# Folding two masks into one, moving q's diagonal copies to GpSimd, and taking eps out of the normalizations' chain

## The chip, the core and the metric

The kernel runs on one core of one Trainium2 chip. A core has a matrix engine (TensorE, PE in the profile; PEld is its weight load), a vector engine (VectorE, DVE), a scalar engine (ScalarE, ACT), GpSimd (POOL), and SyncE (SP), whose queue here issues nearly all DMAs. Each engine takes its instructions in program order; an instruction that waits for a semaphore holds everything behind it on that engine. The metric is the device time of one execution in microseconds; the median of the runs counts.

## What is computed

One transformer block on x of 2048 rows and 448 columns: a normalization modulated by c, attention with 16 heads of 28 columns in a sliding window of 256 keys, a residual, a second modulated normalization, and a gated MLP whose gate mixes all rows (w_sp) after a normalization of its own. Cut to what matters:

```python
def _layernorm(x, axis=-1, eps=1e-05):
    m = jnp.mean(x, axis=axis, keepdims=True)
    v = jnp.var(x, axis=axis, keepdims=True)
    return (x - m) / jnp.sqrt(v + eps)
...
    # A: B, S, D = 1, 2048, 448; H = 16; Dh = 28; W = 256
    scores = jnp.einsum('bhqd,bhkd->bhqk', q, k) * Dh ** (-0.5)
    mask = (idx[:, None] - idx[None, :] >= 0) & (idx[:, None] - idx[None, :] < W)
    scores = jnp.where(mask[None, None], scores, -1000000000.0)
    o = jnp.einsum('bhqk,bhkd->bhqd', _softmax(scores, axis=-1), v)
    return merge_heads(o) @ wo
...
    # B: Fh = 896
    z = _gelu(jnp.einsum('bsd,df->bsf', x, w_in))
    z2 = _layernorm(z[..., Fh:], axis=-1)
    g = jnp.einsum('ts,bsf->btf', w_sp, z2) + b_sp[None, :, None]
    return jnp.einsum('bsf,fd->bsd', z[..., :Fh] * g, w_out)
...
    h = _layernorm(x, axis=-1) * (1 + ca) + sa
    x = x + ga * _A_ref(h, A_wqkv, A_wo)
    h = _layernorm(x, axis=-1) * (1 + cb) + sb
    x = x + gb * _B_ref(h, B_w_in, B_w_sp, B_b_sp, B_w_out)
```

## The kernel before

Rows are tiled by 128 (16 tiles, j or t), and four tiles are a token block (tb 0 to 3). The work of every tile is written as small operations with their dependencies; a class `Sched` holds them. The order is not found at run time: a long string, `PLAN`, lists every operation by number with its engine (p for PE, a for ACT, d for DVE, t for POOL, s for SP) and its buffer slots. `order()` walks it and appends each operation to its engine's program; `waits()` then derives the semaphore waits. The string is one list for all engines, so the place of a word says only what stands before it on the same engine.

The first normalization and Q, K, V (per token block): `stats` runs `bn_stats` (L626) and `bn_aggr` (L629) on DVE, adds eps on DVE or POOL (L631, into `ve_all`), and takes the power -1/2 on POOL (L633, `rs_all`). `norm` normalizes on DVE (L644) or on POOL (L649 the negated mean times rsqrt, into `ve_all` again; L651). SP transposes the result by DMA into `hT` (L467), L732 applies the modulation, and PE makes q (L763; L797 for block 0), k (L821) and v (L841). q is copied from PSUM to `qT` (L772, L773; L802, L803 for block 0). Then four copies per token block put q's heads on a block diagonal, `QBD` (L790 on ACT and L791 on DVE; L815 and L816 for block 0). Each copy writes 32 partitions. They wait for the zeroing of QBD (L521) as well.

Attention for tile j has two halves of 8 heads, each with three key blocks: the middle one needs no mask, the two others (the edges) do. Since they are complementary, they are folded into one 160-column strip per head. The scores of a half go to four PSUM banks (L956), one exponential moves them to `PW` (L912), and DVE multiplies the folded edges by the 0/1 mask into `PT` (L975). This is one operation for four heads, `mask_all(k)`, so two for each half. The scores of 64 further columns of the middle block come from QBD, L967, once per tile. PV (L1003) for four heads, k = 0 or 1 of a half, needs the mask of its k. L1017 and L1019 divide, SP transposes, L1029 multiplies by wo, L1033 adds x, and the second normalization follows for each tile: `stats` with slot 1, `norm` with a copy of the last columns (L656, L657), a transpose by DMA and the modulation (L1052, L1054).

The MLP: L1123 and L1144 are the two parts of x @ w_in, with gelu on ACT (L1130, L1152); z2's normalization uses `stats` with slot 2 (two bn_stats per tile) and L1135. L1168 is w_sp @ z2, L1172 and L1175 the gate, L1187 the output product, L1197 the last residual.

The columns of the folded edges for the two k of a half, before, with `PWT` = 576 columns per PSUM bank's worth:

```python
at_m0, at_f, at_hm = ((0, (128, 288), 448), (384, (64, 224), 0))[j % 2]
...
cols(hp.slot[0] * 2048 + 1024 * k, [[256, 4], [128, 2], [1, 128]]), cols(at_w() + pad + at_f[k], [[PWT, 4], [32, 2], [1, 128]], PW),
cols(0, [[0, 4], [128, 2], [1, 128]], mask01[:].rearrange("p b q -> p (b q)")), ALU.mult), [exs[0]] + t_mask, v - 7.0 + k)
```

Of the kernel before, what the change touches and what calls it, by code (L numbers as in the profile page):

```python
# [12 lines left out]
d24 d22 p47.1 p56.3 p48.2 p55.0 p57.1 p59.0 a0 a3 a5 a7 a9 d23 p37.1 p65.2 p71.3 p61.1 p49.0 p64.2 p50.3 p73.0  # L13
p46.3 p67.0 s1 s2 s4 d110 s6 s10 s8 a38 p42.0 p43 p44.1 p45 p70.2 p72.1 p60.2 t27 t28 t29 t32 t33 t30 d108
d111 t31 d109 t112 t113 t34 a100 t26 t102 t35 d115.3 d114.2 p124.7 d83 d82 p127.0 p75.0 a128 a129 d103 d125
d126 d118 d119 d116 d117 a104 p80.1 p77.0 p78.1 p76.2 p74.0 p52.3 p69.2 p68.0 s12 d182 d180 p62.1 t101 p51.0
p148.1 p81.2 p139.5 p140 p149 a150 p79.1 p54.2 a141 t106 t107 t105 p136.7 p137 a138 p63.2 t120 t121 d123.2
d122.0 p133.3 p130.6 p66.3 p53.0 p145.0 p146 p58.2 a131 d176 d183 d134 a135 s13 d243 d178 d177 d181 d179 t25
d184 t185 t191 t187 t189 d245 d41 d241 d186.3 s11 p142.7 p372.0 a132 p163.1 p170.6 p171 d244 p164 d165 a147
p151.0 p143 d144 d172 d247 p152 d153 a373.0 p378.0 p154.1 p155 d156 a39 a379.4 p397.0 a398.1 a399 a169 t36  # L20
d382 d374 d246 d166 d376 p157.7 p158 a159 s15 p90.1 p91 d92 d248 d84 d85 d242 d400 p93.0 p94 d95 d380 s193
t188.1 s194 t190.2 s195 t192.0 s196 d197 d200 p404.0 a405.5 p173.1 p174 a175 p160.7 p161 p375.0 p86.0 p87 d88
d198 d89 a406 a40 p425.0 a426.6.0 t249 t250 t254 d407 t252 t199 p377 p381 p383 d409 d384 d402 t253.2 d162
p217.0 p218 a219 a168 p210.1 p211 d212 p433.0 a434.0 p201.0 p202 a203 d167 p204.1 p205 a206 s14 d310 d385.2
p401.0 p403 p453.0 a454.2.1 s16 d430 s849 s259 t255.1 s260 d251.0 d256 d429 d436 d312 s386 s258 t257.3 s261
t97 t96 t262 t99 t263 t265 p226.0 p427.0 a428 p207.1 p227 p408 p208 d228 d306 p410 d411 d412.1 d307 s413 d98
d311 d435 a209 d215 d458 p461.0 p229.0 a462.1 d464 d214 d463 d457 p220.1 p221 p230 a231 p431.0 p432 s851
p481.0 p437 p438 d439 p223.0 p224 d225 d313 p455.0 a222 p232.1 d440.2 s441 d213 a482.3.2 d486 p489.0 d308 p233
d234 p235.0 p236 a456 a216 p483.0 p459.0 p460 a490.0 p508.0 d491 d492 d309 s21 s17 s852 p465 p466 d467 d485
d468.0 s469 a237 t264 p387.0 p388 d389 p414.1 p415 a484 p510.0 d416 t314 t315 a509.6.0 p536.0 a511 d390 d512  # L30
d391 p487.0 p488 p493 p494 p272.0 p538.0 d495 d496.1 a537.2.1 d541 d513 d540 p273 a274 p516.0 a517.5 p269.1
p275.0 p276 d277 p270 d271 p514.0 p515 a539 p564.0 a565.3.2 p282.0 p266.1 p267 a268 d519 p283 p566.0 a567 a284
d518 p520 t319 t320.1 s325 t321 t322.2 s326 d316.0 s323 t317 t318.3 s324 t330 d280 d417 d569 p544.0 a545.1
p442.1 p443 d444 d281 p521 d522 d523.0 p288.0 p289 a290 p291.1 p292 a293 p572.0 a573.5 p238.0 p239 d279 p294.1
p542.0 p295 p543 p592.0 a240 p470.0 p471 d445 d446 d546 d418 d419 d278 s20 s497 s848 s524 t392 t393 d547
d394.2 t395 s396 a296 a593.4.0 d568 p548 p549 p285.1 p594.0 p286 a287 p600.0 a601.2 d575 d472 p300.0 p301 a302
d550 d551.1 p570.0 p571 d596 d574 d473 p576 p577 p619.0 t420 t329 t327 d328 d597 p525.1 p337.0 p526 d578
d579.0 p598.0 a595 p599 p338 d603 d474 d527 a620.3.1 p627.0 d602 d528 d475 d421 d529 d530 t531 t447 t476
t422.0 t532 p340.1 p341 a339 s552 p553.0 p554 s18 p604 p605 a628.5 p647.0 a648.6.2 p621.0 a622 d342 p498.1
p499 d555 p297.0 p298 a299 t477 d606 d607.2 d623 p625.0 d624 s853 s580 s608 d500 t423 s424 d652 d556 d630 d557  # L40
d629 d501 t448 t449 t450.1 t451 s452 p675.0 a676.0.0 d680 p626 p334.0 p335 a336 p331.1 p332 a333 d651 d345
t478.2 d479 s480 p655.0 a656.1 p609.0 p610 p649.0 a650 p347.1 p348 p631 a349 d611 d612 d346 d657 d679 d344
p683.0 a684.2 p632 p677.0 d633 d502 p350.0 p351 a352 p359.1 p360 d558 t559 t560 t561.0 t822 t503 d634.2 s635
p703.0 d658 d686 d533.2 p303.0 p304 d305 d685 s19 p653.0 p654 p659 p660 d661 d823 t562 d662.0 s663 t534 s535
t504 t824 t821 d505.1 t506 s507 a704.5.1 p711.0 a361 p353.1 p354 d343 d355 a678 d707 d613 a712.1 d714 d708
p681.0 p365.0 p366 a367 p730.0 a731.3.2 p682 p687 p688 p705.0 a706 d713 d689 d690.2 s691 p356.1 p357 p581.0
a358 d735 d734 p738.0 a739.2 p732.0 a733 p582 d583 d584 p709.0 p710 p715 d740 p716 d717 d718.0 s719 s563 d585
t586 p664.0 p758.0 a759.0.1 p368.1 p369 a370 d741 p665 d666 t587 d588 t589.2 d762 d667 p736.0 p737 p742 p766.0
# [12 lines left out]
d835 t834 d939 d913 d833 d914 d902 d967 d954 d923 d955 d974 d975 t940 t897 d898 d947 t933 d934 t903 t904 d949
# [44 lines left out]
class Op:  # L106
    def __init__(self, n, ways, deps, prio, take, table, dma, lat, tail):
# [1160 lines left out]
```

## Time and profile before

| | |
|---|---|
| median of 3 runs | 282.59 us (282.34 to 283.21) |
| span of the profiled execution, first to last instruction | 279.0 us |
| what lies around the span, median less span | 3.6 us |
| PE, DVE, ACT, POOL busy | 267.3, 164.5, 121.4, 127.3 us |
| the chain that ended last: PE, DVE, POOL, DMA | 53%, 21%, 12%, 7% |
| start of the L1168 stage on the chain | 158.10 us |

The profile lists only the span of its execution, so the time around it is taken from the median. A group's row has the engine's line, the operation, its output and inputs, how often, busy time and mean ns of one, and then the idle time ahead of it with what ended that. A row of a timeline has the start, the time from the first start to the last end of a run of equal instructions, and what it is; in square brackets the idle time ahead. A row of the chain has the start and the share of the chain. DVE's instructions overlap by some 70 ns at their ends, so the distance from start to start is what one costs in a full queue.

### The profile page before, as it was taken

How to read it: one execution, taken by the hardware profiler on the slowest of the kernel's cores; microseconds unless marked ns; L12 is line 12 of the kernel's file. 1: busy time of each engine (PE TensorE's matmuls, PEld its weight loads, DVE VectorE, ACT ScalarE, POOL GpSimd, SP SyncE). 2: the span in 40 equal slices, each digit the busy share in tenths (PEclk: the TensorE clock that was granted, in tenths of full speed). 3: DMA queues.
4: the chain of work that ended last, by engine and by line, in shares of the span. 5: the costliest groups of instructions: out<-in, count | busy, mean ns of one | idle time of the engine just before them, and what ended most of it. 6: DMA issues, size and time to landing. Idle time of an engine off the chain costs nothing.

```text
span 279.0 us, 8426 instructions
## 1 busy us (share of the span) xinstructions
PE 267.3 (96%) x3741; PEld 155.6 (56%) x3751; DVE 164.5 (59%) x377; ACT 121.4 (44%) x142; POOL 127.3 (46%) x182
## 2 busy tenths in 40 slices
PE   7899998998999799999989899999999999999995
PEld 5786686677668676544545444444444444454552
DVE  3698999978999999938879501120212012153143
ACT  2399998899699789466755500000000000000000
POOL 7554567617364831596576503155363024062320
PEclk9999999999999999999999999999999999999999
DMA  7997953956632343659489996000000000102013
GB/s 203 294 238 136 147 100 97 121 93 97 126 62 50 98 80 61 179 89 150 99 153 192 212 182 130 0 0 0 2 1 0 0 2 0 33 16 62 0 39 115
DMA packets 67302, 25.55 MB, mean 92 GB/s; under 512 B 58497, under 2 KB 66178, under 8 KB 67266
## 3 DMA queue, kind: packets, MB, share of 16 engines
q1 hardware_dynamic: 66304, 24.21, 43.6%
q10 hardware_dynamic: 962, 0.80, 1.1%
q8 instruction: 29, 0.48, 0.7%
q14 instruction: 7, 0.06, 0.1%
HBM read 9.01 MB, written 1.84 MB: 39 GB/s over the span
## 4 chain that ended last, share of the span: by engine, by line
PE 53%; DVE 21%; POOL 12%; DMA 7%; ACT 3%; issue 2%; SPq 1%; POOLq 0%; DVEq 0%
PE ps L1168 34%; DVE PT L975 8%; PE ps L1187 8%; POOL rs_all L633 5%; DMA hT<-xn 5%; DVE st_all L626 3%; DMA wmodA<-in_w_mod_dram 2%; DVE o_sb L1019 2%; DVE x_sb L1033 2%; PE ps L763 2%; POOL hT L1054 2%; POOL ve_all L631 2%; PE ps L956 1%; PE ps L821 1%; PE ps L841 1%
## 5 line engine op out<-in xcount | busy, mean ns | idle before, releaser
L1175 POOL TENSOR_TENSOR z1T<-tmpg,z1T 128x512 bf16<-128x512 bf16 x28 | 32.0, 1152 | 74.5 <-DVE tmpg L1172 74.5
L1172 DVE TENSOR_TENSOR tmpg<-ps,bsp_bc 128x512 bf16<-128x512 f32 x28 | 19.0, 689 | 75.6 <-PE ps L1168 64.3
L912 ACT ACTIVATE PW<-ps 128x2048 bf16<-128x2048 f32 (+1 forms) x42 | 60.0, 1454 | 6.8 <-PE ps L956 5.2
L1168 PE MATMUL ps<-wspB,z 128*128 128x512 bf16 x219 | 49.7, 379 | 0.3
L1168 PE MATMUL ps<-wspA,z 128*128 128x512 bf16 x219 | 49.1, 379 | 0.9 <-DVE z L1135 0.7
L975 DVE TENSOR_TENSOR PT<-PW,mask 128x1024 bf16<-128x1024 bf16 x56 | 38.6, 714 | 0.1
L1168 PEld LDWEIGHTS ps<-wspA,z 128*128 128x128 bf16 x224 | 21.8, 98 | 27.2 <-DVE z L1135 1.0
L1168 PEld LDWEIGHTS ps<-wspB,z 128*128 128x128 bf16 x224 | 21.9, 98 | 26.2
L633 POOL TENSOR_TENSOR rs_all<-ve_all,neghalf 128x1 f32<-128x1 f32 (+2 forms) x37 | 24.5, 670 | 19.4 <-DVE ve_all L631 18.3
L1003 PE MATMUL ps<-Vaug,PT 128*128 128x32 bf16 x496 | 23.4, 177 | 1.3 <-DVE PT L975 0.7
L1003 PEld LDWEIGHTS ps<-Vaug,PT 128*128 128x128 bf16 x496 | 21.5, 96 | 3.9 <-DVE o_sb L1019 1.0
L1123 PE MATMUL ps<-w_in,hT 64*128 64x448 bf16 x224 | 22.0, 349 | 1.2 <-DVE st_all L626 1.2
L1144 PE MATMUL ps<-hT,w_in 64*128 64x512 bf16 x196 | 22.2, 376 | 0.0
L1187 PE MATMUL ps<-w_out_g,z1T 128*128 128x448 bf16 (+2 forms) x119 | 22.0, 342 | 0.0
L626 DVE BATCH_NORM_STATS2 st_all<-x_sb 128x6 f32<-128x448 bf16 x32 | 19.5, 617 | 3.0 <-DMA x_sb<-in_A_x_dram 2.8
L626 DVE BATCH_NORM_STATS2 st_all<-z 128x6 f32<-128x448 bf16 x32 | 18.5, 610 | 3.7 <-ACT z L1130 3.6
L1003 PE MATMUL ps<-Vaug,PW 128*128 128x32 bf16 x224 | 19.8, 176 | 0.0
L821 PE MATMUL ps<-hT,WQK 112*128 112x128 bf16 x256 | 17.4, 219 | 1.3 <-DVE KT L834 1.0
L1197 DVE TENSOR_TENSOR fin<-ps,x_sb 128x448 bf16<-128x448 f32 (+2 forms) x17 | 9.8, 595 | 14.7 <-PE ps L1187 9.9
L1003 PEld LDWEIGHTS ps<-Vaug,PW 128*128 128x128 bf16 x224 | 17.5, 96 | 1.1
L956 PE MATMUL ps<-qT,KT 32*128 32x128 bf16 (+5 forms) x1344 | 17.1, 197 | 1.0 <-DVE KT L834 0.9
L1130 ACT ACTIVATE z<-ps 128x896 bf16<-128x896 f32 x16 | 13.9, 914 | 9.3 <-PE ps L1123 6.8
(104 smaller groups left out, 361.8 us busy)
## 6 DMA issues: line engine op xcount, KB each, us to landing
out_dram<-fin SPq DMA_DIRECT2D x15, 112.0 KB, 1.7
wmodB<-in_w_mod_dram SPq DMA_DIRECT2D x1, 1568.0 KB, 14.9
x_sb<-in_A_x_dram SPq DMA_DIRECT2D x3, 448.0 KB, 9.0
w_in<-in_B_w_in_dram SPq DMA_DIRECT2D x3, 448.0 KB, 4.5
w_out_g<-in_B_w_out_dram SPq DMA_DIRECT2D x1, 784.0 KB, 5.0
bsp_bc<-in_B_b_sp_dram SPq DMA_DIRECT2D x1, 512.0 KB, 5.2
x_sb<-in_A_x_dram SPq DMA_DIRECT2D x2, 224.0 KB, 5.1
hT<-xn SPq DMA_TRANSPOSE x28, 3.2
```

The source lines that it names most:

```text
L626: st = [dve(0.62 if True else 0, lambda e, t=t, ci=ci, s=s: e.bn_stats(st_all[:, slot, t, ci, :], s()), deps(t), prio) for ci, s in enumer ...
L633: return pool(0.4 + 0.15 * len(tiles), lambda e: e.tensor_tensor(rs_all[:, slot, a:b], ve_all[:, slot, a:b], neghalf[:, 0:b - a], ALU.pow) ...
L821: km = lambda g, kc, start, stop, h=h, t=t: lambda e: e.matmul(ps[:, h.slot[0], g * 128:(g + 1) * 128], lhsT=WQK[0:CP, kc, 16 + 4 * g:20 + ...
L912: ex = act(xdur, lambda e, out_ap=out_ap, in_ap=in_ap: e.activation(out_ap(), in_ap(), ACT.Exp, scale=SCALE), [s] + list(after), v - 8.0 + ...
L956: fm.append(lambda e, hm=hm, qi=qi, key=key, kn=kn, lo=lo, hi=hi, col=col, p0=p0, t=t, j=j: e.matmul(ps[p0:p0 + kn, hm.slot[t], col:col + ...
L975: return lock_d(0.68, lambda e: e.tensor_tensor(cols(hp.slot[0] * 2048 + 1024 * k, [[256, 4], [128, 2], [1, 128]]), cols(at_w() + pad + at ...
L1003: fns.append(lambda e, hp=hp, hO=hO, hi=hi, bi=bi, kb=kb, hd=hd, nb=nb, a=at[hi][bi], p_of=p_of: e.matmul(ps[:, hO.slot[0], 32 * hd:32 * h ...
L1123: return lambda e, kc, p0, start, stop: e.matmul(ps[:, hs[t % 2].slot[hf], 0:D], lhsT=hT[p0:p0 + 64, kc, t * 128:(t + 1) * 128], rhs=w_in[ ...
L1144: return lambda e, kc, p0, start, stop: e.matmul(ps[:, hs[b // 2].slot[b % 2], :], lhsT=w_in[p0:p0 + 64, kc, ft * 128:(ft + 1) * 128], rhs ...
L1168: m = pe(16 * MMS, [lambda e, h=h, si=si, ft=ft, tb=tb: e.matmul(ps[:, h.slot[0], :], lhsT=z2[:, si, ft * 128:(ft + 1) * 128], rhs=(wspA i ...
L1175: u = pool(1.16, lambda e, ht=ht, ft=ft, tb=tb: e.tensor_tensor(z1T[tb][:, ft, :], tmpg[:, ht.slot[0], :], z1T[tb][:, ft, :], ALU.mult), [ ...
L1187: return [lambda e, ft=ft: e.matmul(ps[:, h.slot[0], 0:hi - lo], lhsT=z1T[t // 4][:, ft, (t % 4) * 128:(t % 4 + 1) * 128], rhs=w_out_g[:, ...
```

## The change

Four edits, and the plan that goes with them.

1. The columns of the folded edges are laid out so that k = 1 lies half a `PWT` behind k = 0 for every bank, and one operation masks all eight heads of a half (128x2048). Both PV of a half wait for it. In the plan it stands in DVE's order where the later one of the two stood, among the same neighbours.
2. `lock_q` lets POOL do the copies to QBD, and the plan gives it the 13 that DVE did; the 3 on ACT stay. As these write 32 partitions, on POOL each such copy waits for the end of the operation before it, and the operation after it waits for the copy (`part`).
3. `st_all` has three more numbers for each normalization, a constant group of zero count and zero mean, and D x eps or Fh x eps as the sum of squares. `bn_aggr` takes it in (9 numbers for 6, or 15 for 12), so its variance has eps in it already; L631 and `ve_all` are gone, and L633 reads bn_aggr's result. Three memsets on DVE at the start write the constants.
4. The negated mean has a tensor of its own, `nm_all`.

The programs of PE, ACT and SP have the same instructions in the same order. On POOL the copies stand: the first ahead of block 1's three L651 and the second between block 2's; for block 1 three of them between the third and the fourth of block 2's L732 (the first copy of that three waits for q on ACT and DVE); for block 2 four of them behind the first of block 3's L732 and ahead of the next L633; for block 3 one ahead of an L651 of the second normalization, two behind it, and the last one behind a run of L1054 and L657.

```diff
+        self.part = False
...
+            prog = self.prog[op.eng]
+            if op.eng == "pool" and prog and (op.part or prog[-1].part):
+                op.deps.add(prog[-1])
+            prog.append(op)
...
-    st_all, _, _ = alloc("st_all", [128, 3, NT, 2, 6], F32)
+    st_all, _, _ = alloc("st_all", [128, 3, NT, 15], F32)
-    ve_all, _, _ = alloc("ve_all", [128, 3, NT], F32)
+    nm_all, _, _ = alloc("nm_all", [128, 3, NT], F32)
...
+    t_eps = [dve(0.1, lambda e: e.memset(st_all[:, :, :, 12:14], 0.0), prio=-98.0),
+             dve(0.1, lambda e: e.memset(st_all[:, 0:2, :, 14:15], D * EPS), prio=-98.0),
+             dve(0.1, lambda e: e.memset(st_all[:, 2:3, :, 14:15], FH * EPS), prio=-98.0)]
...
-            aggr.append(dve(0.2, lambda e, t=t, n=n: e.bn_aggr(mv_all[:, slot, t, :], st_all[:, slot, t, 0:n, :]), st, prio - 0.01))
+            aggr.append(dve(0.2, lambda e, t=t, n=n: e.bn_aggr(mv_all[:, slot, t, :], st_all[:, slot, t, 12 - 6 * n:15]), [st, t_eps], prio - 0.01))
-        fe = lambda e: e.tensor_scalar(ve_all[:, slot, a:b], mv_all[:, slot, a:b, 1], EPS, None, ALU.add)
-        ve = add({"dve": (0.16, fe), "pool": (0.23, fe)}, aggr, prio)
-        return pool(0.4 + 0.15 * len(tiles), lambda e: e.tensor_tensor(rs_all[:, slot, a:b], ve_all[:, slot, a:b], neghalf[:, 0:b - a], ALU.pow),
-                    [ve, t_nh], prio - 0.01)
+        return pool(0.4 + 0.15 * len(tiles), lambda e: e.tensor_tensor(rs_all[:, slot, a:b], mv_all[:, slot, a:b, 1], neghalf[:, 0:b - a], ALU.pow),
+                    [aggr, t_nh], prio - 0.01)
...
     def lock_q(*a):
-        return locks(either(*a))
+        op = locks(free(*a))
+        op.part = True
+        return op
...
-                at_m0, at_f, at_hm = ((0, (128, 288), 448), (384, (64, 224), 0))[j % 2]
+                at_m0, at_f, at_hm = ((160, (0, 288), 448), (224, (64, 352), 0))[j % 2]
...
-                def mask_all(k, hp=hp, at_w=at_w, pad=pad, at_f=at_f):
-                    return lock_d(0.68, lambda e: e.tensor_tensor(
-                        cols(hp.slot[0] * 2048 + 1024 * k, [[256, 4], [128, 2], [1, 128]]), cols(at_w() + pad + at_f[k], [[PWT, 4], [32, 2], [1, 128]], PW),
-                        cols(0, [[0, 4], [128, 2], [1, 128]], mask01[:].rearrange("p b q -> p (b q)")), ALU.mult), [exs[0]] + t_mask, v - 7.0 + k)
-                mks = [mask_all(k) for k in range(2)]
+                mk2 = lock_d(1.2, lambda e, hp=hp, at_w=at_w, pad=pad, at_f=at_f, cols=cols: e.tensor_tensor(
+                    cols(hp.slot[0] * 2048, [[256, 8], [128, 2], [1, 128]]), cols(at_w() + pad + at_f[0], [[PWT // 2, 8], [32, 2], [1, 128]], PW),
+                    cols(0, [[0, 8], [128, 2], [1, 128]], mask01[:].rearrange("p b q -> p (b q)")), ALU.mult), [exs[0]] + t_mask, v - 7.0)
+                mks = [mk2, mk2]
...
-                    at = [[(0, 1024 * k + 256 * hi), (1, PWT * hi + at_m), (0, 1024 * k + 256 * hi + 128)] for hi in range(4)]
+                    at = [[(0, 512 * hi + 256 * k), (1, PWT * hi + at_m), (0, 512 * hi + 256 * k + 128)] for hi in range(4)]
```

The durations in these lines (0.68, 1.2, 0.25 and so on) are the planner's costs, not measurements.

More of the change, by code (lines that the diff above doesn't have):

```diff
@@ L77 @@
+s1070 d1075.0 t1088 p1077.5 s1034 d1123.1 d1066.3 t1124 d1030.2 s1031 d1120.1 t1121 d1078.1 t1079 p1041.4
+d1042.1 s1043 d1036.1 s1067 s1037 p1080.7 p1089.5 p1083.0 d1081.1 t1082 d1084.1 t1115 p1139.2 p1038.1 t1085
+p1135.4 d1090.0 t1091 s1076 d1039.0 s1040 p1140 d1141.0 s1142 p1143.0 p1144 d1145.2 s1146 p1098.3 p1101.6
+d1102.0 d1099.1 s1100 s1103 p1131.5 p1132 p1136 d1133.3 s1134 p1071.2 d1137.0 d1072.2 s1073 s1138 p1104.5
+d1105.3 s1106 p1107.3 d1108.1 s1109
 """
@@ L647, in norm @@
         else:
-            nm = ve_all[:, slot, t:t + 1]
+            nm = nm_all[:, slot, t:t + 1]
             fm = lambda e: e.tensor_scalar(nm, m, z, -1.0, ALU.mult, ALU.mult)
```

129 lines of the change are left out of this document (60 added, 69 removed).

## The prediction

> **What bounds the kernel now.** I read the page's busy table by slices first, then the busy time by stages, then the chain of work that ended last, then the timelines around the points that the change touches. The slices are 7 us each:
>
> ```profile
> DVE  3698999978999999938879501120212012153143
> ACT  2399998899699789466755500000000000000000
> ```
>
> VectorE (DVE) is full from slice 3 to 15 and ScalarE (ACT) nearly so. The stages, cut where the chain changes its engine, say how full each engine is (time, then PE, PE's loads, DVE, ACT, POOL):
>
> ```profile
> 28.20:35.00 6.80, 6.80 (x157) 4.25 (x155) 6.26 (x15) 6.75 (x8) 3.68 (x4) 1.00 1.07 134
> 35.00:56.20 21.20, 20.18 (x621) 15.09 (x618) 20.97 (x43) 18.82 (x19) 14.24 (x16) 1.00 0.62 105
> 75.20:97.70 22.50, 20.94 (x660) 15.94 (x657) 21.61 (x46) 18.93 (x20) 15.15 (x21) 1.00 0.31 66
> 114.40:158.10 43.70, 41.77 (x407) 20.63 (x405) 34.98 (x98) 27.34 (x42) 30.91 (x60) 1.00 0.78 142
> ```
>
> From 28.2 to 35.0 TensorE (PE) has no gap: what starts it late there is lost. From 35.0 to 56.2 DVE is busy 20.97 of 21.20 us and bounds; PE (20.18) and ACT (18.82) are close, so relief of DVE can give 1 or 2 us there, not more. The same holds from 75.2 to 97.7. From 114.4 PE bounds with 1.9 us of gaps, and the last 121 us are PE alone, which the change doesn't touch.
>
> **The change part by part.** The instruction order on PE, ACT and SP is the same before and after. DVE's and POOL's differ. The prices:
>
> ```profile
> L975 DVE TENSOR_TENSOR PT<-PW,mask 128x1024 bf16<-128x1024 bf16 x56 | 38.6, 714 | 0.1
> L996 DVE TENSOR_TENSOR PT<-PT,mask 128x512 bf16<-128x512 bf16 x8 | 3.0, 400 | 0.0
> L791 DVE COPY QBD<-qT 32x512 bf16<-32x512 bf16 x11 | 3.8, 345 | 1.4 <-ACT qT L772 1.2
> L816 DVE COPY QBD<-qT 32x256 bf16<-32x256 bf16 x2 | 0.4, 200 | 0.0
> L631 DVE TENSOR_SCALAR ve_all<-mv_all 128x1 f32<-128x1 f32 x14 | 1.9, 142 | 0.1
> L631 POOL TENSOR_SCALAR ve_all<-mv_all 128x1 f32<-128x1 f32 x18 | 5.9, 334 | 7.4 <-DVE mv_all L629 7.0
> L629 DVE BATCH_NORM_AGGREGATE mv_all<-st_all 128x2 f32<-128x6 f32 x32 | 5.2, 170 | 0.3
> L629 DVE BATCH_NORM_AGGREGATE mv_all<-st_all 128x2 f32<-128x12 f32 x16 | 2.7, 186 | 0.0
> L615 POOL COPY WQK<-wq_st 112x448 bf16<-112x448 bf16 x5 | 2.7, 559 | 2.1 <-DMA wq_st<-in_A_wqkv_dram 2.1
> L657 POOL COPY xn<-xn x13: 231/238/2659, 65.1 to 136.5; 128x64 bf16<-128x64 bf16 x13
> ```
>
> *One mask for two.* No row shows 128x2048. From 512 to 1024 elements a mask grows by 314 ns (714 - 400), so the part that doesn't grow is 86 ns, and 2048 elements should take 714 + 2 x 314 = 1342 ns, against 2 x 714 for the pair: 86 ns x 28 = 2.4 us less. The bounds are 0 (all of it grows) and 28 x 400 ns = 11 us (a whole small mask is fixed), and below nothing if the longer pattern loses speed, which no row gives a reason for. I take 2 us, nearest to the line through both rows, spread evenly from 32 to 113 us. That the first half of a pair comes some 0.6 us later I cost at nothing: PE's program runs each PV some us behind its masks, and that other work covers it. Without the cover it would be 28 x 0.6 us at the most. [...]
>
> *q's diagonal copies.* 13 copies leave DVE: 11 x 345 + 2 x 200 ns = 4.2 us. On POOL two rows give a line: 64 elements in 238 ns, 448 in 559, so 0.84 ns an element, and 512 elements take 0.61 us, 256 elements 0.40. Each also waits for the operation before it on POOL, and the next one for it: some 0.1 us, as between dependent POOL operations below. POOL has room for 8 us in sum. But its queue is in order, so the place of each copy decides.
>
> *First place, the costly one.* The first copy of token block 0 stands in POOL's queue ahead of the three L651 that normalize block 1, and it waits for the last q eviction of block 0, DVE's L803:
>
> ```profile
> 21.75 0.68 DVE L803 CAST qT<-ps 128x512 bf16<-128x512 f32 x1
> 19.04 2.10 POOL L651 TENSOR_SCALAR xn<-x_sb,rs_all,ve_all 128x448 bf16<-128x448 bf16 x3
> 19.80 4.83 SPq L467 DMA_TRANSPOSE hT<-xn  x3
> 25.89 0.74 DVE L732 TENSOR_SCALAR hT<-hT,modT 112x512 bf16<-112x512 bf16 x2
> 28.14 1.05 PE L821 MATMUL ps<-hT,WQK 112*128 112x128 bf16 x16
> DMA to landing us min/median/max: 2.4/3.2/4.9
> ```
>
> Before, the L651 run from 19.04. After, POOL stands until 22.43, copies to about 23.1, and normalizes from 23.2, 4.1 us later. Queued behind on POOL are the next rsqrt and L732; on SP three of the four transposes wait, and behind them loads. The first of the three starts at about 23.9; SP needs 4.83/3 = 1.6 us each while loads fill the DMA, perhaps 1.2 (its lowest here) later: the third starts at 26.3 to 27.1 and lands 2.4 us after, at 28.7 to 29.5. L732 therefore starts 2.8 to 3.6 us late on DVE, of which 0.7 us was a wait for PE in between that is now past. PE's L821, and with it a stretch where PE has no gap, starts **2.1 us** late (2.0 to 2.9).
>
> *Second place.* For block 1 three copies stand behind three L732:
>
> ```profile
> 39.60 0.95 POOL L732 TENSOR_SCALAR hT<-hT,modT 112x512 bf16<-112x512 bf16 x1 [2.57 <-DMA hT<-xn]
> 41.58 3.91 POOL L732 TENSOR_SCALAR hT<-hT,modT 112x512 bf16<-112x512 bf16 x3
> 43.97 0.27 DVE L791 COPY QBD<-qT 32x512 bf16<-32x512 bf16 x1
> 44.41 0.38 PE L967 MATMUL ps<-QBD,KT 128*128 128x256 bf16 x2
> ```
>
> L967 of tile 4 runs at 44.41, right behind the last copy. Before, the first two of the row's three L732 end at 41.58 + 2 x 1.3 = 44.2. After, the DMA ahead of them lands about 0.8 us late (the norms that feed it are 1.4 us late, and SP had slack), so they end at 45.0 and the three copies at 45.0 + 3 x 0.71 = 47.1, less 0.1 after the last. L967 is **2.6 us** late in all, 0.5 more than the first place gave: DVE's relief by then (some 1.3 us) is lost in this wait. Queued behind the copies are the fourth L732 and the rsqrt of block 3, both ahead of need.
>
> *Third place.* For block 2 four copies stand behind the L732 that waits for a transpose, and ahead of the rsqrt that a DVE normalization waits for. This is on the chain that ended last:
>
> ```profile
> 56.24 1.19 SPq L467
> 57.47 4.24 DMA hT<-xn
> 61.80 1.27 POOL hT L732
> 63.15 0.76 POOL ve_all L631
> 63.99 0.58 POOL rs_all L633
> 64.59 0.40 DVE xn L644
> ```
>
> The eps step (0.76 + 0.1) goes. With DVE idle L732 takes its 0.76. Four copies come: 4 x 0.71 = 2.8. Sum at L644: 61.80 + 0.76 + 0.1 + 2.8 + 0.1 + 0.58 = 66.1, against 64.59, so 1.5 more, **4.0 us** late in all. DVE stands, since its other work before L644 gets shorter: the relief here is worth nothing.
>
> *Given back.* From 75.2 to 97.7 DVE bounds and loses four copies and six masks' overhead, 1.8 us; the tile normalizations on POOL lose an eps step each, and PE's 1.6 us of gaps fill. I take the lateness down from 4.0 to **1.8 us** at 92. Then the last copy of block 3 stands behind an L657 that masks starve:
>
> ```profile
> 93.78 2.66 POOL L657 COPY xn<-xn 128x64 bf16<-128x64 bf16 x1
> 94.49 1.85 DVE L975 TENSOR_TENSOR PT<-PW,mask 128x1024 bf16<-128x1024 bf16 x3
> 95.48 0.38 PE L967 MATMUL ps<-QBD,KT 128*128 128x256 bf16 x2
> ```
>
> L657 needs 0.24 us and took 2.66, to 96.44, as long as the masks ran. The copy comes 0.7 us behind it, and L967 of tile 12 at 97.1 on this clock, 1.7 after its turn. As the POOL work ahead is also late and gets shorter, I take 0.9 more: **2.7 us**. [...] From 97.7 to 114.4 PE is full, so little of DVE's relief counts: 2.6 us.
>
> *eps by a constant group.* All 37 L631 go, among them the 14 on DVE and 18 on POOL of the rows above. bn_aggr reads 9 or 15 numbers for 6 or 12: the two L629 rows differ by 16 ns for 6, so 8 ns each, 0.4 us in all. Three small memsets lie where DVE waits for the first load. In the second half this shortens the last normalizations:
>
> ```profile
> L1123 PE MATMUL ps<-w_in,hT 64*128 64x448 bf16 x224 | 22.0, 349 | 1.2 <-DVE st_all L626 1.2
> L1168 PE MATMUL ps<-wspA,z 128*128 128x512 bf16 x219 | 49.1, 379 | 0.9 <-DVE z L1135 0.7
> ```
>
> ```profile
> 156.54 0.74 POOL rs_all L633
> 157.30 0.52 DVE z L1135
> 158.10 10.74 PE ps L1168 x49
> ```
>
> PE's last gap of 0.9 us ends at 158.10 with a z behind a rsqrt behind an L631; three L631 go ahead of it, and 0.15 stay for DVE's own queue of z: 0.75 less. L1123's gap of 1.2 us, at 142, lies behind the last tile's transpose, which starts some 0.45 earlier without the L631 around it. Together **1.2 us less**.
>
> Sum: 2.1 + 0.5 + 1.4 - 2.2 + 0.9 - 0.1 - 1.2 = **+1.4 us** on a span of 279.0. The median of the runs is 282.59, 3.6 above the span; with the same 3.6 the forecast is 284.0.
>
> **The rivals.** *Relief wins (faster).* The waits of the second, third and last place lie in time that the waiting engine has over; only the first stays. Then 2.1 - 2.0 (35 to 56: three copies, seven masks) - 1.8 (75 to 98) - 0.5 - 1.2 = -3.4 at most; with half of the relief kept -1.2; between them -2.3, 280.3 us. It decides at L644: it must not start later than DVE gets there, that is, the four copies must end before the rsqrt's turn. Against it: DVE already waits there 0.8 us. For it: POOL is half idle. *Starved copies (slower).* Each copy waits for a mask of 1.1 to 1.3 us, and stretches others, as L732's three took 3.91 instead of 2.3: three copies at the second place + 1.8, one at the last + 1.2, ten masks stretched by 0.15: 4.5 more than the forecast, 288.5 at most, 286.3 halfway. *Nothing moves.* Losses and gains of some 4 us each cancel within 0.85 us: 282.6.
>
> **How the numbers follow.** 0.3% is 0.85 us, about what a measurement of this kernel can tell from no change. The forecast (283.4 to 285.8) gets 0.40, starved copies 0.18, relief wins 0.27, nothing moves 0.15. So faster 0.27, same 0.15, slower 0.58. The range reaches into both outer cases, from 279.8 (most of the relief kept, and 1 us of the masks' upper bound) to 288.0.
>
> **What would show it.** Right: POOL's first QBD copy after 22.4 and L821 at about 30.2; L967 of tile 4 near 47; DVE idle for 3 us or more before its L644 near 68; L1168 starting near 159.5. Wrong: a mask far from 1.34 us; copies far from 0.61 us; L821 at its old time; or attention (the last PV) ending before 114.

## The result and the profile after

The changed kernel takes **292.34 us** (median of 4 runs, 291.71 to 295.27) against 282.46 us for the kernel before (4 runs, 281.82 to 283.21): a ratio of 1.040, interval 1.033 to 1.048. It is 9.9 us slower, where 1.4 us had been forecast and 288.0 was the upper end of the range. The profiled execution of the kernel after took 292.79 us, with a span of 290.6. Medians in this text are of all executions, while ratios and intervals leave out slow ones (over 1.5% above the fastest of their kernel) and compare with executions of the kernel before made beside the run, whose medians were 281.45 to 282.46 us.

The change shifts the line numbers. The L821, L763, L967, L1123 and L1168 (TensorE) of the prediction are L825, L767, L971, L1124 and L1169 from here on; L975, L732, L644 and L803 are L977, L736, L646 and L807; L633 (rsqrt), L651 (normalization on POOL) and L657 are L635, L653 and L659; L791 and L816 (the copies) are L795 and L820. An L633 is now bn_aggr, an L651 the negated mean. The slices of the page after (7.3 us each) have a row in them that was all nines before:

```profile
DVE  3894789484679896994978921021131101263144
ACT  2699198489758977856676640000000000000000
PEclk9999599799979988999999999999999999999999
```

VectorE (DVE) is no longer full between slices 3 and 15, and TensorE's granted clock falls four times. The same stretches as before, by stage (time; PE, PE's loads, DVE, ACT, POOL; granted clock; DMA share; GB/s):

```profile
28.20:35.00 6.80, 3.34 (x20) 2.15 (x20) 4.09 (x10) 1.56 (x3) 3.04 (x4) 0.55 0.85 201
35.00:56.20 21.20, 17.58 (x500) 12.96 (x500) 15.40 (x28) 16.26 (x16) 16.55 (x15) 0.90 0.45 91
75.20:97.70 22.50, 19.96 (x558) 13.87 (x558) 18.52 (x32) 17.00 (x17) 15.72 (x19) 0.92 0.34 76
114.40:158.10 43.70, 43.57 (x638) 23.29 (x637) 36.17 (x87) 30.54 (x39) 24.57 (x41) 1.00 0.66 122
```

From 28.2 to 35.0 TensorE (PE) was full before; now it works half of the time, and at a granted clock of 0.55. DVE, which was full in the second and third row, has 4 to 6 us over in each: it was relieved, and waits. The mask costs less than estimated (1235 ns for 1342); the copies cost more on average (770 ns for 610), though most took 0.61 us. These are the groups by line and shape (busy us, mean ns of one, idle time before them and what ended it):

```profile
L977 DVE TENSOR_TENSOR PT<-PW,mask 128x2048 bf16<-128x2048 bf16 x28 | 34.3, 1235 | 0.9 <-ACT PW L916 0.8
L736 POOL TENSOR_SCALAR hT<-hT,modT 112x512 bf16<-112x512 bf16 x8 | 10.7, 1345 | 17.0 <-DMA hT<-xn 16.9
L795 POOL COPY QBD<-qT 32x512 bf16<-32x512 bf16 x11 | 8.5, 770 | 0.8
L633 DVE BATCH_NORM_AGGREGATE mv_all<-st_all 128x2 f32<-128x9 f32 x32 | 5.6, 183 | 0.3
L971 PE MATMUL ps<-QBD,KT 128*128 128x256 bf16 x28 | 5.6, 282 | 3.6 <-POOL QBD L795 3.6
L646 DVE TENSOR_SCALAR xn<-x_sb,mv_all,rs_all 128x448 bf16<-128x448 bf16 x11 | 4.6, 437 | 4.7 <-POOL rs_all L635 4.7
L820 POOL COPY QBD<-qT 32x256 bf16<-32x256 bf16 x2 | 0.8, 406 | 3.8 <-DVE qT L807 3.8
```

The last column tells the story: POOL waited 3.8 us for one q eviction, PE 3.6 us for copies, DVE 4.7 us for rsqrts, 3.9 of it for one that stood behind copies.

**First place.** The chain of work that ended last, in order of time, at the first copy:

```profile
20.52 0.69 DVE qT L807
21.89 2.85 POOL xn L653 x3
24.74 0.72 POOL rs_all L635
25.46 4.11 DMA hT<-xn
29.60 1.12 DVE hT L736 x2
30.79 0.66 DVE hT L736
31.66 1.87 PE ps L825 x16
33.53 1.72 PE ps L767 x4
35.27 0.69 DVE qT L777
```

The L653 start at 21.89 and end at 24.74. L736 follows their end by 4.86 us; before it followed by 4.75 (from 19.04 + 2.10 to 25.89). So the whole chain of norms, transposes and L736 is shifted, and nothing in it takes up a part. Then something new: 16 L825 take 1.87 us, where 16 took 1.05, at half the clock.

**Second place.** POOL's timeline, and under it PE's row that waits:

```profile
45.65 2.01 POOL L603 TENSOR_TENSOR wo_g<-wo_g,gg_sb 112x448 bf16<-112x448 bf16 x1
47.65 1.51 POOL L736 TENSOR_SCALAR hT<-hT,modT 112x512 bf16<-112x512 bf16 x2
49.30 2.82 POOL L795 COPY QBD<-qT 32x512 bf16<-32x512 bf16 x3
```

```profile
52.26 0.38 PE L971 MATMUL ps<-QBD,KT 128*128 128x256 bf16 x2 [3.62 <-POOL QBD L795]
```

The last q tile that the copies read was evicted at 41.8 (ACT's L776); the copies stand until 49.30 because the L736 ahead of them in the queue stand: the first starts at 42.72, when its transpose lands, and takes 2.96 us (its row is in the last section).

**Third place.** POOL waits 12.3 us for a transpose, with the four copies queued behind it, whose last q tile had been evicted at 66.3; and DVE's L646 waits for the rsqrt behind the copies:

```profile
70.51 1.00 POOL L736 TENSOR_SCALAR hT<-hT,modT 112x512 bf16<-112x512 bf16 x1 [12.30 <-DMA hT<-xn]
71.57 2.61 POOL L795 COPY QBD<-qT 32x512 bf16<-32x512 bf16 x4
74.27 0.55 POOL L635 TENSOR_TENSOR rs_all<-mv_all,neghalf 128x1 f32<-128x1 f32 x1
```

```profile
74.86 0.40 DVE L646 TENSOR_SCALAR xn<-x_sb,mv_all,rs_all 128x448 bf16<-128x448 bf16 x1 [3.88 <-POOL rs_all L635]
```

**A table by stage.** Executions of one kernel differ here by a per cent or more, and in the traces most of that lies ahead of the first L825, which starts between 9.9 and 14.3 us in kernels whose work up to there is the same. Two profiles of one kernel (all copies well placed, below) show it: L825 first starts at 9.85 and 11.82, the spans are 274.7 and 276.8, and no stage between differs by over 0.25. In the two that start latest (13.8 and 14.3 us, e6 and e7 below) the granted clock stood at 0.50 for 6.8 us from 7.7 and 8.1 us on. So I cut each timeline at the starts of matmuls and compare stages: a, from the first L825 to the first L825 of tile 4 (the first tile of block 1); b, to L971 of tile 4; c, to L971 of tile 8; d, to L971 of tile 12; e, to the first L1169; the rest, 120.9 to 121.2 us, is equal in all. Each number is the difference of two start times in the timeline of PE, in us:

| kernel (run) | a | b | c | d | e | median us |
|---|---|---|---|---|---|---|
| before | 16.83 | 16.28 | 21.26 | 29.81 | 62.62 | 282.46 |
| after | 21.59 | 20.60 | 22.33 | 32.74 | 62.15 | 292.34 |
| all copies on DVE (e1) | 16.78 | 15.61 | 21.72 | 29.14 | 60.81 | 277.57 |
| copies alone on POOL (e2) | 22.32 | 20.73 | 23.44 | 31.66 | 62.49 | 294.50 |
| block 0 on DVE (e3) | 17.16 | 19.01 | 23.51 | 32.76 | 60.83 | 286.67 |
| first copy later (e4) | 16.79 | 19.15 | 22.81 | 32.79 | 62.18 | 286.44 |
| and block 1 placed (e6) | 17.17 | 15.51 | 21.61 | 33.66 | 60.81 | 282.12 |
| e4 with its stall filled (e7) | 17.07 | 19.18 | 21.37 | 33.65 | 61.66 | 286.48 |
| e1 with masks in two (e8) | 16.78 | 16.30 | 21.36 | 31.06 | 61.01 | 280.35 |
| all copies well placed (e5) | 16.78 | 15.51 | 21.61 | 29.23 | 60.80 | 276.60 |
| e5, first place as in after (s1) | 21.85 | 17.31 | 21.60 | 29.38 | 60.81 | 284.87 |
| s1 with its stall filled | 21.73 | 15.38 | 21.60 | 29.27 | 61.00 | 283.58 |
| e5, second place as in after (s2) | 16.88 | 19.20 | 22.39 | 29.20 | 60.81 | 282.65 |
| s2 with its stall filled | 17.20 | 19.13 | 21.37 | 29.22 | 61.25 | 281.62 |
| e5, third place as in after (s3) | 16.78 | 15.50 | 21.60 | 33.44 | 60.81 | 281.44 |
| s3 with its stalls filled | 16.79 | 15.51 | 21.60 | 31.30 | 61.27 | 279.80 |
| e5, last place as in after (s4) | 16.78 | 15.52 | 21.61 | 29.63 | 60.82 | 278.77 |

After against before, the stages give 4.8, 4.3, 1.1, 2.9 and -0.5 us: 12.6 in all. In this pair of profiles an earlier first L825 (10.07 for 11.31 us) took 1.2 off, so the spans differ by 11.6. The medians differ by 9.9, and most of the gap is the profile of before: in every execution that has both numbers listed, the time is 1.7 to 2.2 us above the span, so the one of 279.0 us took some 281 us and was quicker than its median. The 3.6 us "around the span" in the table ahead of the prediction is therefore no time of its own; the forecast adds its 1.4 us to the median and doesn't depend on it.

### The profile page after: what moved, and what is told of

It is laid out like the page before. It is cut to its first block, busy times and chain, and to the rows that moved or that the text cites. A ratio compares the mean times of both kernels' runs of the same rounds, so it can differ in the third digit from the quotient of the medians.

```text
span 290.6 us, 8377 instructions
## 1 busy us (share of the span) xinstructions
PE 273.3 (94%) x3751; PEld 156.7 (54%) x3751; DVE 157.6 (54%) x324; ACT 122.1 (42%) x142; POOL 131.8 (45%) x173
## 4 chain that ended last, share of the span: by engine, by line
PE 72%; POOL 9%; issue 6%; DVE 4%; DMA 4%; ACT 4%; SPq 0%; POOLq 0%; DVEq 0%
PE ps L1169 33%; PE ps L1124 7%; PE ps L1145 7%; PE ps L1188 7%; PE ps L1030 3%; PE ps L1004 3%; PE ps L960 3%; PE ps L825 3%; POOL xn L653 2%; DMA hT<-xn 2%; POOL hT L736 2%; PE ps L767 2%; POOL QBD L795 2%; DMA wmodA<-in_w_mod_dram 2%; PE ps L845 1%
## 5 line engine op out<-in xcount | busy, mean ns | idle before, releaser
L1169 PE MATMUL ps<-wspB,z 128*128 128x512 bf16 x224 | 50.1, 379 | 0.0
L1169 PE MATMUL ps<-wspA,z 128*128 128x512 bf16 x224 | 49.5, 379 | 0.0
L635 POOL TENSOR_TENSOR rs_all<-mv_all,neghalf 128x1 f32<-128x1 f32 (+2 forms) x37 | 24.3, 676 | 27.6 <-DVE mv_all L633 27.4
L1169 PEld LDWEIGHTS ps<-wspA,z 128*128 128x128 bf16 x224 | 21.8, 98 | 26.6 <-issue 0.4
L1169 PEld LDWEIGHTS ps<-wspB,z 128*128 128x128 bf16 x224 | 21.9, 98 | 26.2
L977 DVE TENSOR_TENSOR PT<-PW,mask 128x2048 bf16<-128x2048 bf16 x28 | 34.3, 1235 | 0.9 <-ACT PW L916 0.8
L825 PE MATMUL ps<-hT,WQK 112*128 112x128 bf16 x256 | 18.2, 225 | 5.9 <-DVE modT L557 4.7
L1124 PE MATMUL ps<-w_in,hT 64*128 64x448 bf16 x224 | 22.0, 350 | 0.0
L631 DVE BATCH_NORM_STATS2 st_all<-z 128x6 f32<-128x448 bf16 x32 | 18.4, 607 | 5.8 <-ACT z L1131 5.8
L631 DVE BATCH_NORM_STATS2 st_all<-x_sb 128x6 f32<-128x448 bf16 x32 | 19.4, 615 | 2.6 <-DMA x_sb<-in_A_x_dram 2.4
L825 PEld LDWEIGHTS ps<-hT,WQK 112*128 112x128 bf16 x256 | 15.7, 101 | 7.5 <-POOL xn L653 4.7
L653 POOL TENSOR_SCALAR xn<-x_sb,rs_all,nm_all 128x448 bf16<-128x448 bf16 x17 | 16.1, 950 | 5.8 <-DVE nm_all L651 5.0
L736 POOL TENSOR_SCALAR hT<-hT,modT 112x512 bf16<-112x512 bf16 x8 | 10.7, 1345 | 17.0 <-DMA hT<-xn 16.9
L1153 ACT ACTIVATE z1T<-ps 128x512 bf16<-128x512 f32 x28 | 14.6, 603 | 9.1 <-PE ps L1145 9.1
```

The source lines that it names most:

```text
L631: st = [dve(0.62, lambda e, t=t, o=12 - 6 * (n - ci), s=s: e.bn_stats(st_all[:, slot, t, o:o + 6], s()), deps(t), prio) for ci, s in enume ...
L635: return pool(0.4 + 0.15 * len(tiles), lambda e: e.tensor_tensor(rs_all[:, slot, a:b], mv_all[:, slot, a:b, 1], neghalf[:, 0:b - a], ALU.pow),
L653: on_pool = lambda e: e.tensor_scalar(out(), at(), z, nm, ALU.mult, ALU.add)
L825: km = lambda g, kc, start, stop, h=h, t=t: lambda e: e.matmul(ps[:, h.slot[0], g * 128:(g + 1) * 128], lhsT=WQK[0:CP, kc, 16 + 4 * g:20 + ...
L977: mk2 = lock_d(1.2, lambda e, hp=hp, at_w=at_w, pad=pad, at_f=at_f, cols=cols: e.tensor_tensor(cols(hp.slot[0] * 2048, [[256, 8], [128, 2] ...
L1124: return lambda e, kc, p0, start, stop: e.matmul(ps[:, hs[t % 2].slot[hf], 0:D], lhsT=hT[p0:p0 + 64, kc, t * 128:(t + 1) * 128], rhs=w_in[ ...
```

## The experiments

**Theory A**: the copies' places in POOL's queue cost the time. **Theory B**: the folded mask and the eps group lose too. The first two runs take the change apart.

*All copies back on DVE* (13 words of the order, like this one; the folded mask and eps stay):

```diff
-d246 t167 d374
+d246 d167 d374
```

> All 13 of q's diagonal copies go back to DVE at the same places of the list; the folded mask and the constant eps group stay. Theory A (the copies' places in POOL's queue cost the time): L825 of tile 4 back at 28 to 29 us, no granted clock under 0.9 behind it, L971 of tile 4 at 43 to 45 us, and 278.5 to 281.5 us in all, as the masks give up to 4.3 us of DVE time and eps 1.2 us. Theory B (the folded mask holds the first half of each pair, and the eps group the norms, so these edits lose as well): 284 to 290 us.

277.57 us (276.43 to 278.68), ratio to before 0.986, interval 0.980 to 0.993. B (284 to 290 us) is out, and A's own number (278.5 to 281.5) was too high.

*The copies alone on POOL*, in the kernel before:

```diff
-d246 d166 d376
+d246 t166 d376
```

> The kernel before with nothing changed but the 13 copies, on POOL at the same places. Theory A: 292 to 295 us, since the loss is all the copies' and the other two edits only give. Theory B: 283 to 287 us, since the copies are only a part of the loss and the folded masks, which are twice as long, are what starves POOL.

294.50 us (293.28 to 296.41), ratio 1.048, interval 1.039 to 1.057. The copies make the whole loss, and the two other edits are a gain of some 2 to 5 us. In the table its loss lies in the stages a to d, as that of the kernel after.

*Its place, or its engine?* Two kernels cure the first place in two ways: both copies of block 0 on DVE, or the first one kept on POOL, behind block 1's normalizations:

```diff
-d246 t167 d374
+d246 d374
...
-s195 t192.0 s196
+s195 t192.0 t167 s196
```

> The kernel after with the two copies of token block 0 alone back on DVE. Theory A1 (the first place starts a chain: stall, lower granted clock, late block 1): L825 of tile 4 at 28 to 29 us, L971 of tile 4 at 45 to 47 us, 285 to 288 us in all. Theory A2 (the second and third place set the time whatever the first does): L825 early, but L971 of tile 4 again near 52 us, 290 to 292 us in all.

> The kernel after with the first copy of token block 0 moved behind the three normalizations of block 1 in POOL's queue; it stays on POOL. Theory A1 (its place costs, not its engine): within 1 us of the kernel with both block 0 copies on DVE, 285 to 288 us, L825 of tile 4 at 28 to 29.5 us. Theory C (a copy on POOL costs by itself, by contention with DVE for SBUF): 289 to 292 us.

286.67 us (ratio 1.017, 1.009 to 1.025) and 286.44 us (1.018, 1.011 to 1.025): the same time, and stage a is back at 17.16 and 16.79. It is the place: theories A2 and C, both from 289 or 290 us up, are out. But the second place then stalls PE on its own (b is still 19.0 and 19.2), and the clock falls there instead. Windows of 2 us in the kernel with the first copy later:

```profile
42.00:44.00 2.00, 0.47 (x9) 0.30 (x6) 1.03 (x3) 1.96 (x2) 1.84 (x3) 1.00 0.29 66
44.00:46.00 2.00, 0.00 (x0) 0.00 (x0) 1.16 (x2) 0.00 (x0) 1.90 (x2) 0.54 0.89 249
46.00:48.00 2.00, 1.67 (x50) 1.53 (x50) 0.00 (x0) 0.60 (x1) 1.90 (x3) 0.50 1.14 230
48.00:50.00 2.00, 2.00 (x63) 1.25 (x52) 0.83 (x2) 1.48 (x1) 1.70 (x5) 0.50 0.04 8
50.00:52.00 2.00, 2.00 (x28) 0.97 (x30) 1.93 (x4) 0.45 (x2) 1.90 (x3) 0.75 0.00 0
52.00:54.00 2.00, 2.00 (x99) 1.70 (x87) 2.00 (x5) 1.97 (x2) 0.17 (x1) 1.00 0.49 112
```

PE stands from 42.5 to 46.3; 1.7 us into that its clock is halved, and it comes back 4.7 us after PE has work again.

*All copies on POOL, each where its q tile is ready and POOL has room.* To the edit above come block 1's three copies ahead of the first L736, block 2's four ahead of the L736 that waits for a transpose, and block 3's last right behind the one before it:

```diff
-s260 t100 t99 t261 t102
+s260 t100 t99 t215 t214 t213 t261 t102
...
-s322 t328 t279 d414
+s322 t279 t280 t278 t277 t328 d414
...
-d628 d648 t342 p651.0
+d628 d648 t342 t341 p651.0
```

> All 13 copies stay on POOL, but stand where their q tile is ready and POOL has room: block 0's first behind the three normalizations of block 1, block 1's three ahead of its three L736, block 2's four ahead of the L736 that waits for a transpose, block 3's last right behind the one before it. Theory A (the place costs, not the engine): no stall over 1.5 us before L825 and L971 of tile 4, granted clock 1.00 all through, 275.5 to 279 us. Theory C (a copy on POOL costs by itself, as masks on DVE hold it up or it holds them up, 0.3 to 0.6 us each): 281 to 285 us.

276.60 us (276.43 to 278.93), ratio 0.985, interval 0.980 to 0.990. The copies are no cheaper there (second row below), yet the clock stays at full and no matmul waits for them, so theory C (281 to 285 us) is out here too:

```profile
PEclk9999999999999999999999999999999999999999
```

```profile
L795 POOL COPY QBD<-qT 32x512 bf16<-32x512 bf16 x11 | 8.8, 802 | 4.3 <-ACT qT L776 3.6
```

*Block 0 and block 1 placed alone*, blocks 2 and 3 as in the kernel after:

> As the kernel with block 0's first copy moved, and block 1's three copies ahead of its three L736 as well; blocks 2 and 3 as in the kernel after. Theory A (second place: a stall of 4.0 us before L971 of tile 4, and some 6.8 us at half the granted clock behind it): 280 to 282 us, no half clock near 46 us. Theory D (the third place then holds DVE's L646 to the same time): 285 to 287 us.

282.12 us (281.04 to 285.19), ratio 1.006, interval 1.001 to 1.010. b falls to 15.51, as in the well placed kernel, and c with it: the third place does not hold that time (theory D is out). What is left is in d, but for 0.4 us in a.

*The stall filled.* 17 matmuls of no use run in the stall of 3.9 us of the kernel with the first copy later:

```diff
-a449 a216 p473.0
+a449 a216 p1147.0 p473.0
...
+    t_keep = pe(0.0, [lambda e: e.matmul(ps[:, hF.slot[0], :].rearrange("p (a b) -> p a b", b=128), lhsT=fill[:],
+                                         rhs=fill[:].unsqueeze(1).broadcast_to([128, 4, 128]), start=True, stop=True) for _ in range(17)], [t_fill], 0.0, [hF])
```

> As the kernel with block 0's first copy moved, with 17 matmuls of no use (128x512, into the bank that L971 takes next) put into TensorE's stall of 4.0 us ahead of L971 of tile 4. The stall stays; if an idle TensorE is what lowers the granted clock, it stays at 1.00 near 46 us. Theory E (the clock costs time of its own): 283 to 285 us against 286.4. Theory F (behind the stall DVE and ACT bound, so a slower TensorE costs nothing): 286 to 287 us.

286.48 us (285.28 to 289.89): by the time alone theory F, nothing gained. The stages say more: c falls from 22.81 to 21.37, and d, which the third place sets, rises by 0.86, as the clock fell there for 6.8 us (76.3 to 83.2) instead of 3.4 (74.9 to 78.3). This run doesn't settle it, since a second stall lies behind the filled one, and the profiled execution began late (first L825 at 14.31); it is made again below with one place at a time.

*Masks in two*, the kernel with all copies on DVE, each folded mask as two operations of 1024 elements:

> As the kernel with all copies on DVE, but each folded mask issued as two masks of 1024 elements, one behind the other, in the new layout: what is left of the change is the eps group and the order. Theory G (the fixed part of the masks is worth time): 28 x 0.15 us more of DVE work, half or more of it on the path, 279.5 to 282 us against 277.6. Theory H (masks lie beside PE's work, and the gain is that of the eps group and of shorter POOL chains): 277 to 278.5 us.

280.35 us (278.42 to 281.77), ratio 0.996, interval 0.993 to 1.000. By the stages the split costs 0.7 in b and 1.9 in d, less 0.4 in c: 2.4 us with e. Theory G holds. A part of d is the clock again: it stands at half for 3.4 us from 69.9, behind a stall of 1.35 us.

**Each place by itself.** The kernel with all copies well placed, with one place put back as in the kernel after. Theory I: the places add up. Theory K: the stages behind take the delay up. L and M dispute what is in d.

> The kernel with all copies well placed (276.6 us), with block 0's first copy alone put back to the first place, ahead of the three normalizations of block 1. Theory I (the places add up): 276.6 + 5.9 = 282.5 us, as taking this place out of the kernel after gave 5.9; L825 of tile 4 at 31 to 32 us, granted clock 0.5 behind it. Theory K (the stages after it take most of the delay up, and it was the sum of places that cost): 278 to 280 us.

> As the kernel with all copies well placed, with block 1's three copies alone put back behind their three L736. Theory I (places add up): 276.6 + 4.3 = 280.9 us; L971 of tile 4 some 19 us after L825 of tile 4 instead of 15.5, granted clock 0.5 behind it, and no loss after L971 of tile 8. Theory K: 277 to 279 us.

> As the kernel with all copies well placed, with block 2's four copies alone put back behind the L736 that waits for a transpose. Theory L (this place carries the 4.4 us that the stage from L971 of tile 8 to L971 of tile 12 is longer with blocks 2 and 3 as in the kernel after): 279.5 to 281.5 us, with the clock under 1.00 near 73 to 78 us. Theory M (the last place carries it): 276.5 to 278 us.

> As the kernel with all copies well placed, with block 3's last copy alone put back behind the L659 that the masks hold up. Theory L: 276.5 to 278.5 us. Theory M: 279.5 to 281.5 us, L971 of tile 12 some 33 us after L971 of tile 8 instead of 29.2.

These took 284.87 (ratio 1.013, 1.005 to 1.020), 282.65 (1.005, 1.002 to 1.008), 281.44 (1.001, 0.998 to 1.005) and 278.77 us (0.991, 0.986 to 0.995). By the stages against the well placed kernel the four cost 7.0 + 4.6 + 4.2 + 0.4 = **16.2 us**; the kernel after and the well placed one differ by 15.5 in the same stages. The places add up: theory I, with larger prices than I gave the first two, and L by the stages, with the third place as nearly the whole of d (the 278.77 us lie between L's range and M's). K is out: nothing behind a place gives anything back. That the two sums agree to 0.7 us is in part luck. In the kernel after, d is longer by 3.5 us, not by the 4.7 of the single places, since the clock fell there for 3.4 us instead of 6.8; and e is longer by 1.35, behind a fall at 107.3 us that no single place shows.

**The wait and the clock.** Theory E: the half clock behind a stall costs time of its own. Theory F: it does not, since DVE and ACT bound there. The same three kernels with their stalls filled by 22, 17, and 4 and 7 matmuls of no use:

> As the kernel with the first place alone wrong (284.87 us), with 22 matmuls of no use (128x512) in TensorE's stall of 5 us before L825 of tile 4. Theory E (the half clock behind the stall costs time of its own: L825 and L767 took twice their time): granted clock 1.00, 282 to 283.5 us. Theory F (the stage behind is bound by DVE and ACT): 284.3 to 285.5 us.

> As the kernel with the second place alone wrong (282.65 us), with 17 such matmuls in the stall of 4.1 us before L971 of tile 4. Theory E: granted clock 1.00, L971 of tile 8 21.4 us after that of tile 4 instead of 22.4, 281 to 282 us. Theory F: 282.3 to 283 us.

> As the kernel with the third place alone wrong (281.44 us), with 4 and 7 such matmuls in the stalls of 1.2 and 1.6 us near 65 and 68 us. Theory E: granted clock 1.00 from 69 to 76 us, L971 of tile 12 about 32 us after that of tile 8 instead of 33.4, 279.5 to 280.5 us. Theory F: 281 to 282 us.

283.58, 281.62 and 279.80 us, by 1.3, 1.0 and 1.6 less than with the stalls left empty. PE in the kernel with the first place alone put back, and then with its stall filled:

```profile
33.92 1.86 PE L825 MATMUL ps<-hT,WQK 112*128 112x128 bf16 x16 [4.92 <-DVE modT L557]
35.58 1.91 PE L767 MATMUL ps<-hT,WQK 112*128 112x512 bf16 x4
```

```profile
28.21 4.91 PE L1208 MATMUL ps<-fill 128*128 128x512 bf16 x22
33.16 1.05 PE L825 MATMUL ps<-hT,WQK 112*128 112x128 bf16 x16
34.05 1.03 PE L767 MATMUL ps<-hT,WQK 112*128 112x512 bf16 x4
```

The wait is the same (a is 21.85 and 21.73), the work behind it takes half. The stages give the clock's share: 17.31 - 15.38 = 1.9 us at the first place, 22.39 - 21.37 = 1.0 at the second, 33.44 - 31.30 = 2.1 at the third. So **5.0 of the 16.2 us are the clock**, and 11.2 the waits, by one execution of each. Theory E holds. Stages a and e of the filled kernels are up to 0.5 longer, for a reason that stays open; over all five stages 3.9 us are won, by the medians 4.0. The other executions say the same of the clock: in all 30 of the three filled kernels its mean was at least 0.998, in 23 of the 24 of the unfilled ones it was 0.987 to 0.994.

*The well placed kernel again*, as a base beside these:

> The kernel with all copies well placed on POOL once more, as the base for the three and for a closer comparison with the kernel before: 276 to 278 us, ratio 0.980 to 0.990. If the earlier 276.6 us was luck: 278 to 280 us.

277.79 us (276.56 to 279.34), ratio 0.988, interval 0.983 to 0.993. It beats the kernel before by 1.2 to 1.5%, as does the one with all copies on DVE (ratio 0.986); those two are not told apart. Against before, the stages give the well placed kernel 2.9 us; the medians give 3.7 to 5.0. A part of the rest is the clock again, which fell in some executions of before but not in the profiled one: of 72 that count for the ratios, 44 had a mean of at least 0.998 and averaged 280.8 us, 28 had 0.992 to 0.994 and averaged 281.8; the seven of the well placed kernel that kept it average 277.0. What is left would lie ahead of the first L825, where one profile of before is not enough to say: that stays open.

## Why the prediction was wrong, step by step

- **What bounds: the reading was right, its use was not.** "What starts it late there is lost" was said of PE at 28.2, and held for every place. But later lateness was set off against DVE's relief ("given back", -2.2 us). No stage shows any of that: s1, s2 and s3 have c, d and e of the well placed kernel to 0.2 us wherever their own place does not lie. A delay of PE's in-order program stayed in these runs.
- **One mask for two: right, too small.** 1235 ns was measured for 1342 estimated. DVE's mask work falls from 38.6 to 34.3 us, and splitting it again costs 2.4 us of the path (a part of it the clock), for 2 forecast.
- **A copy's price: right.** Undisturbed ones take 0.61 us and follow one another every 0.66, as the four of the third place (2.61 in all). The mean of 770 ns comes of some that took 1.50.
- **First place: the step that failed first**, 2.1 us forecast. The L653 start 4.1 us late against the first L825 (21.89 - 10.07 and 19.04 - 11.31), as worked out. But the three took 2.85 us for 2.10, and the last transpose was timed from SP's turn with the shortest landing (2.4 us), when in the trace L736 follows the third normalization by 4.75 us. That row stood in the fence, unused. Of the 0.7 us taken off for a wait for PE, only 0.2 came back (L825 follows L736 by 2.06 us, for 2.25 before). The wait is 5.1 us (s1), and **the lower granted clock behind it, which the prediction does not mention, adds 1.9**.
- **Second place: mis-sized**, 0.5 us forecast, 3.5 of wait measured, and 1.0 of clock. The step took it that most of DVE's relief and of the first place's delay would be spent in the same wait. They add: with the first place cured PE still waits 3.9 us for the copies. With it uncured, the transpose ahead of the first L736 landed 3.1 us later by the clock of the trace (42.72 for 39.60), where the step had 0.8. One of the three copies took 1.50 us while a mask ran, which is the second rival's mechanism.
- **Third place: right in kind**, down to DVE's stand ("DVE idle for 3 us or more": 3.88), 1.4 us forecast, 2.1 of wait measured, and 2.1 of clock that were not foreseen.
- **Last place:** 0.9 us forecast, 0.4 measured (s4).
- **eps by a constant group: right.** 1.2 us forecast; stage e is 1.6 to 1.8 us shorter (62.62 to 61.01 with the masks in two, 60.81 with them folded), and both of PE's gaps are gone: the idle time ahead of L1124, 1.2 us before, is 0.0. No run has the eps edit alone; the kernel with the masks in two comes nearest.
- **The rivals.** Relief wins is what the kernel gives when the places are cured (276.6 and 277.8 us, where the rival said 280.3). Starved copies, at 288.5 at most, was the nearest in time, but its mechanism shows in two copies at most. No run shows every copy waiting for a mask: in the kernel after nine of the eleven copies of 512 elements took 0.61 us, the two others 1.50 (at the second place) and 1.52 (the last copy), both while a mask ran.

With the measured terms the sum is 16.2 - 2.9 = 13.3 us by the stages, for 12.6 found.

## What to carry to other kernels

A move to an idle engine is priced by what stands ahead of the moved operation in that engine's queue when its data arrive, and by what it then stands ahead of; the engine's idle share says nothing about it. Where a full TensorE gets a stall of some 1 us or more, look at the granted clock behind the stall and price it as a term of its own: here it fell to 0.50 behind stalls of 0.66 to 4.9 us, though not behind each, and that made 5.0 of the 16.2 us above. Before such a move is given up, put each moved operation where its input is ready and the queue is not waiting for something else: the same 13 copies cost 15 us in one order, and in another nothing that these runs can tell from leaving them on DVE.

## What the runs showed of the hardware

**The granted clock falls behind short stalls, and in steps.** It went to 0.50 in stalls of 4 to 5 us (at 28.8 us in the kernel after, at 44.2 in the one with the first copy later), and also behind two of 1.08 and 1.43 us (the third place alone), behind one of 1.35 us (masks in two), at 107.3 us in the kernel after behind one of 0.93 us, and at 102.2 in the one with the first copy later behind one of 0.66. Stalls of 1.02 and 1.21 us in the kernel before, two of 0.59 and 0.92 us in a row there, and one of 1.11 us with the last place alone left it at full. So no length of one stall decides it in these traces. In the kernel after the clock steps at 28.84, 35.66, 52.73, 56.14, 80.04, 83.45, 107.34 and 110.76 us, each step 1, 2, 5 or 7 times 3.41 us behind the one before. TensorE's busy share in the 3.41 us that end where the clock makes its steps sorts them better. Between 16 and 160 us of the traces, 16 of 18 falls follow such a window with 0 to 60% busy (1.68 of 3.41 us from 65.36 in the third place alone, 2.06 from 66.45 in masks in two); the other two, at 107.3 and 102.2 us above, follow one with 70% (2.39 us). In every window of the same grid behind which the clock stayed at full, it was 64% or more (2.21 us from 139.86 in the kernel before). Each of these falls lasted 3.4 us (52.7 to 56.1 in the kernel after) or 6.8 (28.8 to 35.7). The steps lie differently against the work from one execution to the next: at the third place the fall came 1.4 us after the second stall began in the kernel after (80.0 and 78.6), and 0.6 us after with that place alone (68.8 and 68.1), and lasted 3.4 and 6.8 us. Windows of the third place alone:

```profile
66.00:68.00 2.00, 1.53 (x40) 1.54 (x40) 1.97 (x4) 1.86 (x2) 2.00 (x3) 1.00 0.33 74
68.00:70.00 2.00, 0.57 (x22) 0.47 (x18) 2.00 (x4) 0.66 (x2) 2.00 (x1) 0.69 0.39 66
70.00:72.00 2.00, 2.00 (x66) 1.38 (x63) 1.33 (x5) 0.66 (x1) 0.06 (x1) 0.50 0.64 192
72.00:74.00 2.00, 2.00 (x24) 0.99 (x23) 0.30 (x1) 1.22 (x1) 0.00 (x0) 0.50 1.19 204
74.00:76.00 2.00, 2.00 (x63) 1.03 (x60) 2.00 (x4) 0.60 (x1) 0.00 (x0) 0.60 0.22 38
```

With fillers in the stalls the clock stayed at 1.00 (a mean of at least 0.998 in all 30 executions, for 0.987 to 0.994 in 23 of the 24 without), so in these kernels it was TensorE's idle time that lowered it.

**POOL's operations stretch while masks run on DVE.** In the kernel after an L736 that takes 0.77 us where it is shortest took 2.96, as three masks ran one behind the other (POOL, then DVE):

```profile
42.72 2.96 POOL L736 TENSOR_SCALAR hT<-hT,modT 112x512 bf16<-112x512 bf16 x1 [1.55 <-DMA hT<-xn]
```

```profile
42.89 3.86 DVE L977 TENSOR_TENSOR PT<-PW,mask 128x2048 bf16<-128x2048 bf16 x3
```

This was read in several places and not tried by itself, so that the masks are the cause is not shown; the well placed kernel shows it too (three copies in 3.10 us) and loses nothing by it, as nobody waits.
